# A fused mLSTM, token mixer and gated MLP on one core: the first two transfers are issued by ScalarE instead of SP

## The chip, the cores and the metric

The kernel runs on one core of one Trainium2 chip. The metric is the device time of one execution in microseconds (us). A core has TensorE (PE, whose weight loads are listed apart as PEld), VectorE (DVE), ScalarE (ACT), GpSimd (POOL) and SyncE (SP). Each has a queue of its own and works through it in order. Transfers between HBM and the core's memory (DMA) are issued by an instruction on an engine's queue and then run by themselves; whoever needs the data waits for a semaphore.

## The reference

Three stages on 2 sequences of 768 tokens, cut to what matters:

```python
# 1. mLSTM, 8 heads of 40: a recurrence with gates, in float32
for t in range(S):
    m_new = np.maximum(f_gate[:, :, t] + m, i_gate[:, :, t])
    f_stab, i_stab = np.exp(f_gate[:, :, t] + m - m_new), np.exp(i_gate[:, :, t] - m_new)
    m = m_new
    C = f_stab[..., None, None] * C + i_stab[..., None, None] * np.einsum('bhd,bhe->bhde', vt, kt)
    n = f_stab[..., None] * n + i_stab[..., None] * kt
    y[:, :, t] = sigmoid(o_gate[:, :, t]) * np.einsum('bhde,bhe->bhd', C, qt) / np.maximum(abs(n . qt), 1)
# 2. mixer: over tokens, then over channels
u  = x + (np.maximum(x.T @ w_tok1, 0) @ w_tok2).T
x2 = u + np.maximum(u @ w_ch1, 0) @ w_ch2
# 3. gated MLP: h = gelu(x2 @ w_in); u, v = halves of h; v normalized, mixed over tokens by w_sg
out = x2 + (u * (w_sg @ v_n + b_sg)) @ w_out
```

The mixer's weights come as float64 words and are made float32 on the chip.

## The kernel before, in words

The recurrence is done in chunks of 128 tokens, 6 for each of the 2 sequences, 12 in all (n = 0 to 11). First the gates of all chunks are worked out once (function gates): a scan on DVE over the f gates (L578), small transposes and matmuls on PE, and factors that are spread over heads (LR at L595 and L596, MR at L611). A chunk then has three parts. p1 makes the decay matrix E of 128 x 1024 in two halves: a matmul (L700), exp on ACT (L701), a mask on POOL (L702). p2 multiplies keys and queries on PE (L712) and the product with E on DVE (L713). p3 updates the carried state (L738, L743, L747, L751, L755), scales the queries with a row that is read back from DRAM (qs = wb x qk, L735; for chunk 1 from PE, L728) and makes the chunk's output (L761, L763, L764 to L768) in nat. The first token-mixing matmul of a chunk (L804) follows. After six chunks of a sequence come the second one (L836 to L838), transposes (L817, L820), and from about 95 us on the channel mixing and the gated MLP, long runs of matmuls.

Transfers: gates_in (gin: gates and small masks) and con (identity and masks) come first, both from one DRAM tensor (L544, L545). Each chunk loads qk in three pieces (L690 twice, L692) and kvo (L682), into three sets of buffers (qk, kvo: NSET = 3). Parts of the qk buffers that the transfers don't write are set to zero once at the start (L561 on DVE for the first set and on POOL for the others, L562 on POOL). wq goes out to DRAM once for each sequence (L650) and comes back in three pieces a chunk (wb, L733). Weights are loaded and converted in to_f32: the transfer (L499), ACT takes the absolute value (L503), DVE does four steps (L504 to L510), then ACT and POOL or DVE split it (L518, L519). rw__133 and rw__135 hold the first token weights, rw__136 and rw__138 the second.

The order on each queue isn't that of the code. Every operation is first recorded in a plan with an estimated cost; the planner simulates the engines from these estimates with several settings, takes the best of the orders that it finds, and issues that. A transfer is given an issue cost on its engine and a place in one common DMA queue; at most eight transfers are in flight, since each takes one of eight lanes (DMAHW0 to DMAHW7) and waits until the transfer eight before it has landed. Element-wise work marked flex may go to DVE or to POOL. Where the simulated PE would stand idle before it first uses a certain bank, the planner puts fillers there (matmuls on a constant, L576).

Of the kernel before, what the change touches and what calls it, by code (L numbers as in the profile page):

```python
# [424 lines left out]
def tile_mlstm_mixer_gmlp(  # L425
# [21 lines left out]
    pe, act, dve, pool, sp = (Engine(plan, e) for e in ("PE", "ACT", "DVE", "POOL", "SP"))  # L447
# [8 lines left out]
    def sb(name, col, n, dt=F32):  # L456

        t = nc.alloc_sbuf_tensor_at(name, [128, n], dt, offset=origin + 4 * col).ap()
        plan.base[t.tensor.name] = col
        return t  # L460
# [5 lines left out]
    con = sb("con", CON, 268)  # L466
# [74 lines left out]


    gates_in = r_gate.take("gin", 293)
    sp.dma_start(out=gates_in, in_=gates_d[:, 0:293])  # L544
    sp.dma_start(out=con, in_=gates_d[:, 293:561])  # L545
    fg, ig = gates_in[:, 0:128], gates_in[:, 128:256]
    ind12, neg, cap = gates_in[:, 256:268], gates_in[:, 268:269], gates_in[:, 269:270]
    ind6, hm = gates_in[:, 270:276], [gates_in[:, 276 + 8 * b:284 + 8 * b] for b in range(B)]
# [645 lines left out]
```

## Time and profile before

| | us |
|---|---|
| runs | 358.65, 359.51, 362.36 |
| median | 359.51 |
| profiled execution | 358.93 |
| its span, first to last instruction | 357.2 |
| PE busy | 350.1 (98%) |
| weight loads (PEld) busy | 337.8 (95%) |
| DVE, ACT, POOL busy | 258.0, 164.3, 96.2 |

The profiled execution is longer than its span by 1.7 us, which lie before the first and behind the last instruction. Busy times of one engine can include pipelining: a PE that is shown busy isn't at its peak. SPq, POOLq and so on stand for an engine's own queue, where transfers are issued and semaphores awaited. A buffer's number is left out of its name, so that wb stands for either of two buffers and ps for every bank of PSUM.

### The profile page before, as it was taken

The numbers are of one execution on the slowest core, as the hardware profiler recorded it, in microseconds if no ns is written. First come the engines' busy times: TensorE is split into PE (matmuls) and PEld (weight loads), VectorE is DVE, ScalarE is ACT, GpSimd is POOL, SyncE is SP. The second block draws the span as 40 slices with busy tenths as digits, with TensorE's granted clock in tenths as the row PEclk, the third lists the DMA queues.
The fourth block names the chain that finished last, engine by engine and source line by source line (L and its number), as shares of the span: only waits on it lengthen the run. The fifth ranks groups of instructions, "written<-read, shape, count | busy, mean of one in ns | idle before, by whom it ended". The sixth has DMA issues, their size and how long they took to land.

```text
span 357.2 us, 5949 instructions
## 1 busy us (share of the span) xinstructions
PE 350.1 (98%) x2238; PEld 337.8 (95%) x2238; DVE 258.0 (72%) x505; ACT 164.3 (46%) x367; POOL 96.2 (27%) x109
## 2 busy tenths in 40 slices
PE   8999999999999999999999999999999999999996
PEld 7889989989999999999999999999999999999995
DVE  5898789998896448981863468788799887455463
ACT  5677537864644235431442348545544544222230
POOL 4345337344223001110010005864231534000100
PEclk9999999999999999999999999999999999999999
DMA  5968777967900002001650000000000010010101
GB/s 155 322 199 305 229 230 263 306 235 237 333 4 0 2 9 111 0 3 44 242 171 0 2 1 2 0 0 2 1 2 0 0 57 0 2 56 1 57 0 55
DMA packets 12698, 32.47 MB, mean 91 GB/s; under 512 B 1766, under 2 KB 5694, under 8 KB 12670
## 3 DMA queue, kind: packets, MB, share of 16 engines
q1 hardware_dynamic: 12670, 32.10, 27.4%
q8 instruction: 17, 0.28, 0.3%
q14 instruction: 11, 0.09, 0.1%
HBM read 30.08 MB, written 2.02 MB: 90 GB/s over the span
## 4 chain that ended last, share of the span: by engine, by line
PE 81%; DMA 11%; DVE 3%; SPq 2%; issue 1%; POOL 1%; ACT 0%; DVEq 0%; POOLq 0%
PE ps L873 6%; PE ps L871 6%; PE ps L872 6%; PE ps L858 5%; PE ps L857 5%; PE ps L856 5%; PE ps L1028 5%; PE ps L1027 5%; PE ps L1026 5%; DMA qk<-in_qk_dram 4%; DMA rw__135<-in_tok_dram 4%; PE ps L763 2%; PE ps L861 2%; PE ps L860 2%; DMA rw__138<-in_tok_dram 2%; PE ps L1044 2%
## 5 line engine op out<-in xcount | busy, mean ns | idle before, releaser
L807 ACT ACTIVATE a<-ps 128x384 fp32r<-128x384 f32 x48 | 23.5, 491 | 53.6 <-PE ps L861 53.1
L808 DVE SCALAR_TENSOR_TENSOR a<-ps,a 128x384 fp32r<-128x384 f32 x48 | 26.6, 555 | 26.2 <-ACT a L807 25.7
L1028 PE MATMUL ps<-wsg,v 128*128 128x384 f32 x96 | 32.3, 336 | 0.0
L1026 PE MATMUL ps<-wsg,v 128*128 128x384 f32 x96 | 32.3, 336 | 0.0
L1027 PE MATMUL ps<-wsg,v 128*128 128x384 f32 x96 | 32.2, 336 | 0.0
L811 DVE TENSOR_TENSOR nat<-ps,nat 128x320 f32<-128x320 f32 x48 | 22.3, 489 | 13.8 <-PE ps L873 8.6
L712 PEld LDWEIGHTS ps<-qk 120*128 120x128 f32 (+1 forms) x192 | 24.9, 191 | 2.0 <-DVE nat L768 0.8
L712 PE MATMUL ps<-qk 120*128 120x128 f32 (+1 forms) x192 | 26.2, 275 | 0.5 <-DMA qk<-in_qk_dram 0.5
L1032 ACT CAST gs<-g 128x384 fp32r<-128x384 f32 x16 | 8.2, 512 | 37.2 <-DVE g L1031 37.2
L763 PE MATMUL ps<-kvo,E 128*128 128x41 f32 x192 | 23.2, 279 | 0.0
L702 POOL TENSOR_SCALAR_AFFINE_SELECT E<-E 128x512 f32<-128x512 f32 x24 | 17.9, 755 | 19.2 <-ACT E L701 18.1
L763 PEld LDWEIGHTS ps<-kvo,E 128*128 128x128 f32 x192 | 22.7, 192 | 0.0
L973 ACT ACTIVATE sq<-ps 128x384 f32<-128x384 f32 (+1 forms) x28 | 15.0, 535 | 14.5 <-PE ps L991 9.9
L974 DVE SCALAR_TENSOR_TENSOR sq<-sq,ps 128x384 f32<-128x384 f32 (+1 forms) x28 | 16.9, 608 | 6.5 <-ACT sq L973 6.0
L1030 DVE SCALAR_TENSOR_TENSOR g<-ps,gln,bsg 128x384 f32<-128x384 f32 x16 | 9.9, 617 | 15.5 <-PE ps L1028 15.5
L975 ACT ACTIVATE sq<-sq 128x384 f32<-128x384 f32 (+1 forms) x28 | 15.7, 568 | 9.8 <-DVE sq L974 9.5
L1028 PEld LDWEIGHTS ps<-wsg,v 128*128 128x128 f32 x96 | 18.0, 188 | 0.2 <-POOL v L1001 0.2
L1026 PEld LDWEIGHTS ps<-wsg,v 128*128 128x128 f32 x96 | 18.0, 188 | 0.0
L1027 PEld LDWEIGHTS ps<-wsg,v 128*128 128x128 f32 x96 | 18.0, 188 | 0.0
L824 DVE TENSOR_TENSOR uT<-ps,uT 128x384 fp32r<-128x384 f32 x24 | 13.3, 552 | 6.2 <-ACT uT L823 6.0
L701 ACT ACTIVATE E<-ps 128x512 f32<-128x512 f32 x24 | 14.2, 593 | 7.4 <-PE ps L700 6.2
L713 DVE TENSOR_TENSOR E<-ps,E 128x512 f32<-128x512 f32 x24 | 16.2, 683 | 2.0 <-PE ps L712 1.4
(351 smaller groups left out, 1118.4 us busy)
## 6 DMA issues: line engine op xcount, KB each, us to landing
kvo<-in_kvo_dram SPq DMA_DIRECT2D x12, 504.0 KB
qk<-in_qk_dram SPq DMA_DIRECT2D x36, 120.0 KB
rwin<-in_win_dram SPq DMA_DIRECT2D x5, 512.0 KB
rwsg<-in_wsg_dram SPq DMA_DIRECT2D x6, 384.0 KB
out_dram<-nat SPq DMA_DIRECT2D x12, 160.0 KB
rwo<-in_wout_dram SPq DMA_DIRECT2D x4, 320.0 KB
wb<-wq SPq DMA_DIRECT2D x18, 60.0 KB
rw__133<-in_tok_dram SPq DMA_DIRECT2D x1, 768.0 KB
```

What stands on the lines that cost most here:

```text
L702: pool.affine_select(out=E[:, hf], in_=E[:, hf], pattern=[[0, 4], [1, 128]], compare_op=ALU.is_ge, fill=0.0, base=0, channel_multiplier=-1)
L712: mm(p[:, j, :], kt[jj][0:r, g, :], qt[0:r, g, :], start=True, stop=True)
L763: mm(psO[:, h, :], E[:, h // 4, h % 4, :], v1[:, h, :], start=(c == 0 and h == 0), stop=(h == H - 1))
L807: act.activation(out=hi, in_=p, func=AF.Relu)
L808: dve.scalar_tensor_tensor(out=lo, in0=p, scalar=0.0, in1=asf(hi), op0=ALU.max, op1=ALU.subtract)
L811: dve.tensor_tensor(out=nat[:, b, s], in0=p, in1=nat[:, b, s], op=ALU.add)
L871: mm(acc, a[:, 0, js], w[:, 0, :], start=(m == 0), stop=False)
L872: mm(acc, a[:, 0, js], w[:, 1, :], start=False, stop=False)
L873: mm(acc, a[:, 1, js], w[:, 0, :], start=False, stop=(m == 5))
L1026: mm(p, v[:, 0, ds_], wsg[s][:, 0, ts], start=(s == 0), stop=False)
L1027: mm(p, v[:, 0, ds_], wsg[s][:, 1, ts], start=False, stop=False)
L1028: mm(p, v[:, 1, ds_], wsg[s][:, 0, ts], start=False, stop=(s == NC - 1))
```

## The change

Two lines name another engine for the issue.

```diff
     gates_in = r_gate.take("gin", 293)
-    sp.dma_start(out=gates_in, in_=gates_d[:, 0:293])
-    sp.dma_start(out=con, in_=gates_d[:, 293:561])
+    act.dma_start(out=gates_in, in_=gates_d[:, 0:293])
+    act.dma_start(out=con, in_=gates_d[:, 293:561])
```

Since the planner's simulation starts from other queues, it settles on another order for every engine. Three places show it.

**The start.** ACT's queue from its first instruction on, as a difference (+ is new):

```order
 L1189 UNCONDITIONAL_BRANCH
+L544 DMA gin<-in_gates_dram 128x293
+L545 DMA con<-in_gates_dram 128x268
 L581 ACT_TABLE_LOAD
 L581 ACTIVATE gt<-gt 128x128
```

The two transfers now stand ahead of the table load. SP's queue starts with the qk pieces of chunk 0 (L690 twice, L692), which stood third to fifth before, and its following issues keep their order up to the second piece of the fifth qk load. DVE's queue at the same place:

```order
 L1189 UNCONDITIONAL_BRANCH
-L561 MEMSET qk 120x384
 L575 MEMSET gt 128x128
 L626 MEMSET gt 1x1
+L561 MEMSET qk 120x384
 L578 SCALAR_TENSOR_TENSOR gt<-gt,gin 128x128
```

The zeroing of the first qk buffer, for which the first qk transfer waits, has moved behind the two memsets of the gates.

**The first chunk.** DVE's queue at the end of the gates' work, as a difference; L596 writes LR for the later chunks, L713 makes E of chunk 0, L611 spreads the factors for the chunks after it:

```order
 L652 TENSOR_SCALAR gt<-gin,gt 128x12
-L596 SCALAR_TENSOR_TENSOR LR<-LR,gin,ps 128x512
-L713 TENSOR_TENSOR E<-ps,E 128x512 x2
 L606 TENSOR_SCALAR gt<-gt 64x128
 L607 SCALAR_TENSOR_TENSOR gt<-gt 64x128
 L611 TENSOR_TENSOR MR<-gt,gin 128x512 x2
+L596 SCALAR_TENSOR_TENSOR LR<-LR,gin,ps 128x512
+L713 TENSOR_TENSOR E<-ps,E 128x512 x2
 L647 TENSOR_TENSOR wq<-gt,wq 64x128
```

L606, L607 and two L611 now come before L713. PE's queue over the same stretch, before:

```order
L655 MATMUL ps<-gt,selr 120x12 x3
L712 MATMUL ps<-qk 128x128 x10
L743 MATMUL ps<-wv,kvo 120x3x41 x2
L700 MATMUL ps<-MR,LR 128x512
L743 MATMUL ps<-wv,kvo 120x2x41
L763 MATMUL ps<-kvo,E 128x41 x4
```

and now:

```order
L655 MATMUL ps<-gt,selr 120x12 x3
L712 MATMUL ps<-qk 128x128 x4
L700 MATMUL ps<-MR,LR 128x512
L712 MATMUL ps<-qk 128x128 x2
L576 MATMUL ps<-gt 128x128 x3
L743 MATMUL ps<-wv,kvo 120x3x41
L700 MATMUL ps<-MR,LR 128x512
L743 MATMUL ps<-wv,kvo 120x3x41
L712 MATMUL ps<-qk 128x128 x4
```

The L712 work of chunks 0 and 1 is split, the first matmul for E (L700) comes earlier, and three fillers (L576) stand ahead of L743. Over the whole queue there are 10 fillers before and 17 now: one more at the start, these three, and three more ahead of the first L761.

**Weights and qs, some 25 to 50 us in.** SP's queue from rw__136 on, before:

```order
L499 DMA rw__136<-in_tok_dram 128x1536
L499 DMA rw__138<-in_tok_dram 128x1536
L650 DMA wq_87<-gt 8x6x128
L690 DMA qk<-in_qk_dram 40x768 x2
L692 DMA qk<-in_qk_dram 40x2x384
L733 DMA wb<-wq_86 40x256
L733 DMA wb<-wq_86 40x384 x2
L690 DMA qk<-in_qk_dram 40x768 x2
L692 DMA qk<-in_qk_dram 40x2x384
L682 DMA kvo<-in_kvo_dram 128x1008
```

and now, some ten rows behind rw__136:

```order
L682 DMA kvo<-in_kvo_dram 128x1008
L733 DMA wb<-wq_86 40x256
L733 DMA wb<-wq_86 40x384 x2
L690 DMA qk<-in_qk_dram 40x768 x2
L692 DMA qk<-in_qk_dram 40x2x384
L682 DMA kvo<-in_kvo_dram 128x1008
L499 DMA rw__138<-in_tok_dram 128x1536
L650 DMA wq_87<-gt 8x6x128
L690 DMA qk<-in_qk_dram 40x768 x2
L692 DMA qk<-in_qk_dram 40x2x384
L682 DMA kvo<-in_kvo_dram 128x1008
```

rw__138 and the second wq have moved back, behind three more qk loads, two kvo loads and six wb loads. POOL's queue over the same chunks, before:

```order
L755 TENSOR_TENSOR nb<-cd,ct 120x328
L702 AFFINE_SELECT E<-E 128x512 x2
L768 TENSOR_TENSOR nat<-tn,dn 128x320
L702 AFFINE_SELECT E<-E 128x512 x4
L738 TENSOR_TENSOR wv<-kvo,wT 128x328
L702 AFFINE_SELECT E<-E 128x512 x2
L735 TENSOR_TENSOR qs<-wb,qk 120x384
L702 AFFINE_SELECT E<-E 128x512 x2
```

and now:

```order
L755 TENSOR_TENSOR nb<-cd,ct 120x328
L702 AFFINE_SELECT E<-E 128x512 x2
L738 TENSOR_TENSOR wv<-kvo,wT 128x328
L735 TENSOR_TENSOR qs<-wb,qk 120x384
L702 AFFINE_SELECT E<-E 128x512 x3
L735 TENSOR_TENSOR qs<-wb,qk 120x384
L702 AFFINE_SELECT E<-E 128x512
L735 TENSOR_TENSOR qs<-wb,qk 120x384
L702 AFFINE_SELECT E<-E 128x512 x4
L735 TENSOR_TENSOR qs<-wb,qk 120x384
```

Of the nine qs operations (L735) eight were on DVE and one on POOL; now three are on DVE and six on POOL, between the masks L702. ACT's L503 on rw__138 stood behind the 12th L701 and the third L764, and now stands behind the 14th and the fifth.

## Rows read from the trace of the kernel before

**Rows 1.** the page, part 4: shares of the chain that ended last

```profile
PE 81%; DMA 11%; DVE 3%; SPq 2%; issue 1%; POOL 1%; ACT 0%; DVEq 0%; POOLq 0%
```

**Rows 2.** busy us by stretch: PE PEld DVE ACT POOL; clock, DMA share, GB/s

```profile
10.00:100.00 90.00, 88.01 (x660) 81.36 (x658) 80.58 (x155) 56.16 (x146) 36.44 (x41) 1.00 0.79 261
100.00:350.00 250.00, 250.00 (x1511) 244.96 (x1510) 170.20 (x327) 102.02 (x209) 54.92 (x56) 1.00 0.08 27
```

**Rows 3.** all that PE waited for: us in total, times, longest; six rows

```profile
PE ps L576 <- DVE gt L626: 1.5, 1, 1.5
PE ps L700 <- ACT E L701: 0.9, 3, 0.4
PE ps L712 <- DMA qk<-in_qk_dram: 0.5, 1, 0.5
...
PE ps L743 <- POOL wv L738: 0.2, 1, 0.2
```

**Rows 4.** groups of 0 to 100 us; then the chain, start us, us, what

```profile
L712 PEld LDWEIGHTS ps<-qk 120*128 120x128 f32 x144 | 20.4, 191 | 2.0 <-DVE nat L768 0.8
...
79.28 1.15 PE ps L804 x4
```

**Rows 5.** timeline, first 4 us: start, us, engine, line, operation [idle before]

```profile
0.78 1.28 ACT L581 ACT_TABLE_LOAD   x1 [0.78 <-PEq L1178]
...
0.79 0.38 SPq L544 DMA_DIRECT2D gin<-in_gates_dram  x1
0.94 0.38 DVE L561 MEMSET qk<- 120x384 f32 x1 [0.94 <-PEq L1178]
1.22 0.41 SPq L545 DMA_DIRECT2D con<-in_gates_dram  x1
1.29 0.17 DVE L575 MEMSET gt<- 128x128 f32 x1
...
1.68 0.74 SPq L690 DMA_DIRECT2D qk<-in_qk_dram  x2
2.08 0.31 ACT L581 ACTIVATE gt<-gt 128x128 f32<-128x128 f32 x1
...
2.46 0.94 SPq L692 DMA_DIRECT2D qk<-in_qk_dram  x1
...
3.14 0.42 DVE L578 TENSOR_TENSOR_SCAN gt<-gt,gin 128x128 f32<-128x128 f32 x1 [1.68 <-DMA gin<-in_gates_dram]
...
3.48 0.49 ACT L642 CAST selr<-con 128x360 fp32r<-128x360 f32 x1 [1.09 <-DMA con<-in_gates_dram]
```

**Rows 6.** timeline around chunk 0 on DVE and PE

```profile
11.94 0.69 DVE L713 TENSOR_TENSOR E<-ps,E 128x512 f32<-128x512 f32 x1 [0.42 <-PE ps L712]
...
13.11 1.80 DVE L611 TENSOR_TENSOR MR<-gt,gin 128x512 fp32r<-128x512 f32 x2
...
15.21 1.02 PE L763 MATMUL ps<-kvo,E 128*128 128x41 f32 x8
```

**Rows 7.** SP's queue: waits; then the chain between 4 and 45 us

```profile
SPq L690 <- DMA rw__138<-in_tok_dram: 2.6, 1, 2.6
...
27.53 7.53 DMA rw__138<-in_tok_dram
```

**Rows 8.** timeline of SP and of ACT around L503 on rw__138

```profile
38.46 0.36 SPq L682 DMA_DIRECT2D kvo<-in_kvo_dram  x1
...
43.70 0.18 ACT L764 ACTIVATE dn<-ps 128x8 f32<-128x8 f32 x1 [1.29 <-PE ps L763]
...
45.96 0.58 ACT L701 ACTIVATE E<-ps 128x512 f32<-128x512 f32 x1
```

**Rows 9.** tile wb: ns min/median/max, first, last start; who waited

```profile
L735 DVE TENSOR_TENSOR qs<-wb,qk x8: 551/558/980, 28.4 to 78.2; 120x384 f32<-120x384 f32 x8
...
L735 POOL TENSOR_TENSOR qs<-wb,qk x1: 1011/1011/1011, 51.8 to 51.8; 120x384 f32<-120x384 f32 x1
...
  DVE qs L735: 1.3, 2
```

## The prediction

> **What bounds the kernel now.** I read the chain of waits [rows 1], busy time by stretch [rows 2], all that PE waited for [rows 3], and then the timeline at the places that the change touches [rows 5 to 8]. 81% of the chain that ended last is PE. Behind 100 us PE is busy in 250.00 of 250.00 us and its weight loads in 244.96 [rows 2]: nothing that happens at the start can shorten that part, only begin it earlier or later. The granted clock is 1.00 in both stretches, so no term below is a clock term. The question is when PE gets through the first 100 us.
>
> How much could be won there? The named waits of PE are six and add up to 3.6 us, from 1.5 down to 0.2 [rows 3]; the 1.5 us stand before anything can run. That leaves 2.1 us.
>
> The Trainium skill ("Perfetto Trace Analysis", section "Identifying the Most-Contended Engine") warns against this reading: pipelined matmuls make TensorE's busy share a bad measure, and that of weight loads is to be used. The trace shows the difference: between 10 and 100 us PE has 88.01 of 90 us, the loads 81.36 [rows 2], so by that rule 8.6 us are open and not 2.1.
>
> From rows alone: 90 − 81.36 = 8.6 us without a load are no stall where a matmul takes longer than the next load. A load takes 0.191 us, an L804 matmul on the chain 1.15/4 = 0.29 [rows 4]; 48 of them hide 48 × 0.10 = 4.8 us. 3.8 us are left, the L700 matmuls still in it. So a reordering of the first 100 us gains 2.1 to 3.8 us at the very most: 1%, and only if every stall goes.
>
> **The change part by part.** The sum is made on the profiled execution: 358.93 us, 357.2 of span and 1.7 around it. The median of the three runs is 359.51, 0.6 higher.
>
> *SP loses two issues.* gin and con took 0.38 and 0.41 us there, and the first qk issue started at 1.68 [rows 5]; without them SP could start at 0.79. But that qk issue also waits for the DVE memset of its tile (L561), and the planner has moved this memset behind two others. From DVE's first start at 0.94, L575 (0.17), the one-element L626 and L561 (0.38) end near 1.55. SP starts some 0.1 us earlier, not 0.9, and its next 20 issues keep the old order; kvo of chunk 0 still waits for gin. Gain 0 to 0.1 us. That the change does not do what it says is thus part of my forecast.
>
> *ACT gets two issues ahead of its table load.* At SP's prices they end at 0.79 + 0.38 + 0.05 + 0.41 = 1.63, the load (1.28) at 2.91, the first ACTIVATE (0.31) at 3.22. L642, next on ACT, started at 3.48, when con had landed [rows 5]: 0.26 us to spare. gin is issued at the old time, so the DVE scan that waits for it stays at 3.14. Were an issue on ACT as dear as the dearest of these rows, 0.94, gin would leave 0.56 us later and con 1.09, and L642 with it. An issue that cost nothing would bring gin 0.4 us earlier. I take SP's figures, since they are for the same two transfers.
>
> What would a late gate chain cost? E of chunk 0 was ready at 11.94 + 0.69 = 12.63, and PE used it at 15.21 [rows 6], behind the work on kvo. The plan now puts L606, L607 (half a microsecond together by the gap of 12.63 to 13.11) and two L611 (1.80) ahead of both halves of E: 2.3 us, so E is ready near 14.9 and 0.3 us of cover are left. A chain late by 1.1 us costs 0.8; on time it costs nothing. Behind this cover every further microsecond counts in full.
>
> *A second DMA queue.* All issues before came from SP, so no trace shows ACT's queue. con may now share the DMA engines with qk. It landed 3.48 − 1.63 = 1.85 us after its issue; shared with one other transfer that could double, at the worst 1.85 us late, 1.5 us behind the cover. At the best it saves nothing, since it was first in line before. I take 0: qk is issued when con is already under way.
>
> The Trainium skill ("DMA: Bandwidth & Descriptors", section "Issuing engines are not separate DMA queues") says that transfers issued from any engine run on the same 16 DMA engines, and that several issuers save only sequencer time. By it the gain is at the most the 0.84 us of SP's issuing; no run here shows it yet.
>
> *The planner's new order.* This is the larger part: every engine is rearranged up to 100 us.
>
> First, seven more fillers (L576) stand in PE's queue, six of them among the work of chunks 0 to 2. Each makes two records; at one load each (0.191 [rows 4]) that is 6 × 2 × 0.191 = 2.3 us if none lies in a gap, and nothing if all do. The first three stand right in front of L743, which waited for wv before. I take +0.2.
>
> Second, rw__138 leaves SP seventeen issues behind rw__136 and not right behind it. Before, a qk issue waited 2.6 us for the lane that it held, and 7.53 us of the chain are its transfer [rows 7]. That wait goes. Late next is PE's own loop: there PE waited for E alone, 0.9 us in three times [rows 3]. So 0 to −0.9; I take −0.3. In exchange ACT's L503 on rw__138 now stands behind the fourteenth E and the fifth L764, which ran at 43.70 [rows 8]. The transfer is issued right behind kvo of chunk 6, at 38.46 before; with its 7.53 us it lands near 46. ACT would stand 2 us there, with two E's queued behind it, but the next E started only at 45.96 anyway. With L503's 0.9 us that E comes 1 us late: 0 to +1.0, and I take +0.2.
>
> Third, qs = wb × qk (L735): eight of nine were on DVE at 0.56 us, one on POOL at 1.01 [rows 9]; now three are on DVE and six on POOL. Five move: 5 × 0.45 = 2.3 us if each is on the path. Against that POOL has 53.6 of 90 us idle [rows 2] and DVE is relieved by 2.8 us. I take +0.3.
>
> The sum: 358.9 + 0 + 0.2 − 0.3 + 0.2 + 0.3 = 359.3. On the median's scale it is 359.9; I say **359.4 us**, a change too small to see.
>
> **The rivals.** *Faster, 356.8 us:* SP's queue is the limit of the first 50 us, and without the wait on rw__138 all named waits of PE behind the start vanish: 358.9 − 2.1. For it: the new order drops a link of 7.53 us from the chain. Against: PE waited for a transfer just once, 0.5 us [rows 3].
>
> *Slower, 365.1 us:* POOL's queue blocks. Each L735 waits for its wb transfers, and now the masks (L702) of later chunks' E stand behind it; where wb lands after ACT has finished that E, POOL stands, E is late, and PE with it. The price is the 2.3 us above and the wait that DVE had for wb, 1.3 us in two cases [rows 9], 0.65 each, six times: 3.9. Together 358.9 + 6.2. For it: POOL works in order, and five of the six stand directly ahead of an L702. Against: with rw__138 out of the way wb lands earlier, and E is made several chunks ahead.
>
> *ACT late, 360.2 us:* issues on ACT cost 0.94 each, the gate chain is 1.1 us late, and the forecast's 359.4 grows by 0.8. For it nothing in the rows but that no issue on ACT was ever seen; against it that SP's issues of the same shape took 0.4.
>
> The Trainium skill ("ScalarE: Activation LUTs", section "What ACT_TABLE_LOAD costs") counts a drain of about 1.38 us to each load; by it L642 would come some 1.1 us late, the same 360.2. The trace speaks against it: the load began at 0.78, took 1.28, and the ACTIVATE began at 2.08 [rows 5].
>
> **How the numbers follow.** The three runs spread over 3.7 us, so about 1% is what a measurement of this kernel tells from no change. The forecast, within 1.5 us of 359.4, gets 0.70, the faster rival 0.10, the blocked POOL 0.13, ACT late 0.07. Faster by over 1%, under 355.9, needs every stall of the larger count to go: 0.05. Over 363.1 lies most of the POOL case, and a little of the fillers on top of another loss: 0.12. Within 1%: 0.83. The range goes from the faster rival, 356.8, to 363.2, where fillers and half of the POOL price would come together; the rest of the POOL case is left out.
>
> **What would show it.** Right: the first qk issue near 1.6, L642 near 3.5, PE's first L763 near 15.2, the qk issue near 33 without its wait, PE's named waits still some 2 us behind the start, and the same 245 us of loads in the last 250. Wrong: L642 after 4.3, so that ACT's issue is dear; L702 late behind an L735 that waits for wb, with PE's wait for E over 3 us in sum; ACT standing at L503 beyond 47. The forecast fails if PE reaches its first steady stretch, near 95 us, more than 3 us earlier or later than before.

## The result, and the profile after

The changed kernel takes 361.26 us (median of 20 runs, 358.53 to 368.2), the kernel before 358.01 beside it (20 runs). The ratio is 1.0071, 95% interval 1.0048 to 1.0093: slower, by 1.7 to 3.3 us. The forecast of 359.4 said no change; the median lies in its range, and 0.71% in its "within 1%", but it is a change that a measurement does tell from none. The median lies in the range by the range's width, which is luck, and not by the sum, which gave 0.4 us. The comparison leaves disturbed executions out, and the profiled one of the changed kernel (365.42 us, span 363.6) is one of these; it shows the loss larger than it is on average.

First the start, on the timeline of the changed kernel (start, us, engine, line, operation):

```profile
0.78 0.39 ACTq L544 DMA_DIRECT2D gin<-in_gates_dram  x1
...
1.20 0.45 ACTq L545 DMA_DIRECT2D con<-in_gates_dram  x1
1.52 0.75 SPq L690 DMA_DIRECT2D qk<-in_qk_dram  x2
1.68 1.28 ACT L581 ACT_TABLE_LOAD   x1 [1.68 <-PEq L1178]
...
2.97 0.31 ACT L581 ACTIVATE gt<-gt 128x128 f32<-128x128 f32 x1
...
3.18 0.42 DVE L578 TENSOR_TENSOR_SCAN gt<-gt,gin 128x128 f32<-128x128 f32 x1 [1.68 <-DMA gin<-in_gates_dram]
...
3.48 0.49 ACT L642 CAST selr<-con 128x360 fp32r<-128x360 f32 x1 [0.20 <-DMA con<-in_gates_dram]
```

Against [rows 5] this is as forecast: two issues at SP's price (0.39 and 0.45 us), SP's first qk 0.16 us earlier, the scan at the same time, L642 at 3.48 as before. The start isn't where time is lost. All that PE waited for, as [rows 3] has it for before:

```profile
PE ps L700 <- ACT E L701: 3.8, 1, 3.8
PE ps L576 <- DVE gt L575: 1.1, 1, 1.1
PE ps L761 <- DVE qs L728: 0.9, 1, 0.9
PE ps L817 <- DVE nat L811: 0.2, 1, 0.2
```

Three waits for E of 0.9 us together have become one of 3.8, and 0.9 for L728 is new. The timeline around the long one, SP's rows first:

```profile
38.86 0.41 SPq L682 DMA_DIRECT2D kvo<-in_kvo_dram  x1
39.32 0.42 SPq L499 DMA_DIRECT2D rw__138<-in_tok_dram  x1
39.78 0.68 SPq L650 DMA_DIRECT2D wq<-gt  x1
...
48.59 2.17 SPq L733 DMA_DIRECT2D wb<-wq  x6
...
43.61 0.18 ACT L764 ACTIVATE dn<-ps 128x8 f32<-128x8 f32 x1 [1.58 <-PE ps L763]
...
45.44 0.50 DVE L738 TENSOR_TENSOR wv<-kvo,wT 128x328 f32<-128x328 f32 x1 [3.30 <-PE ps L700]
48.42 0.90 ACT L503 ACTIVATE wt<-rw__138 128x768 f32<-128x768 f32 x1 [4.64 <-DMA rw__138<-in_tok_dram]
49.22 0.58 ACT L701 ACTIVATE E<-ps 128x512 f32<-128x512 f32 x1
49.85 0.79 PE L700 MATMUL ps<-MR,LR 128*128 128x512 f32 x1 [3.85 <-ACT E L701]
...
52.93 3.34 PE L763 MATMUL ps<-kvo,E 128*128 128x41 f32 x15
```

rw__138 is issued at 39.32 and lands at 48.42, after 9.1 us instead of 7.53 [rows 7]. ACT stands 4.64 us at L503, the E behind it comes at 49.22 (before: 45.96, [rows 8]), and PE stands. Two more engines stand in the same stretch: DVE at L738 until 45.44, and SP, whose six wb wait for wq until 48.59. (The releaser that the DVE row names had been done long before; in e0 and e2 below the same row names kvo.) Busy time by stretch, columns as in [rows 2]:

```profile
40.00:50.00 10.00, 6.15 (x49) 5.61 (x47) 6.59 (x14) 3.19 (x9) 2.15 (x4) 0.93 0.79 234
50.00:60.00 10.00, 10.00 (x45) 9.04 (x45) 5.49 (x10) 1.72 (x5) 2.35 (x4) 0.55 0.48 144
60.00:100.00 40.00, 39.69 (x305) 37.11 (x304) 36.17 (x70) 26.67 (x69) 17.51 (x17) 1.00 0.76 254
100.00:350.00 250.00, 250.00 (x1514) 244.93 (x1513) 175.57 (x337) 104.21 (x216) 49.40 (x53) 1.00 0.10 35
```

Behind the pause the granted clock is 0.55 for ten us, the lower of its two levels (1.2 of 2.4 GHz) for most of them, and 15 L763 take 3.34 us. The last stretch is as before: 244.93 us of loads, 244.96 in [rows 2].

Where PE is at the end of the recurrence tells how much is lost by then. Its last group of L804 but one, before (first row) and after (second):

```profile
93.85 0.70 PE L804 MATMUL ps<-nat,w__134 128*128 128x320 f32 x2
```

```profile
100.53 0.70 PE L804 MATMUL ps<-nat,w__134 128*128 128x320 f32 x2
```

From there to the end it is 357.2 − 93.85 = 263.35 us before and 363.6 − 100.53 = 263.07 after. So the whole loss is ahead of this mark, in every run below but e7. The mark is used for all of them.

### The profile page after: what moved, and what is told of

The parts are those of the page before. It is cut to its first block, busy times and chain, and to the rows that moved or that the text cites. A ratio compares the mean times of both kernels' runs of the same rounds, so it can differ in the third digit from the quotient of the medians.

```text
span 363.6 us, 5982 instructions
## 1 busy us (share of the span) xinstructions
PE 354.0 (97%) x2252; PEld 342.3 (94%) x2252; DVE 262.9 (72%) x507; ACT 163.3 (45%) x367; POOL 91.2 (25%) x107
## 4 chain that ended last, share of the span: by engine, by line
PE 87%; DMA 5%; DVE 4%; issue 1%; SPq 1%; ACT 1%; ACTq 0%; DVEq 0%
PE ps L873 6%; PE ps L871 6%; PE ps L872 6%; PE ps L858 5%; PE ps L857 5%; PE ps L856 5%; PE ps L1028 5%; PE ps L1027 5%; PE ps L1026 5%; PE ps L763 4%; PE ps L712 3%; PE ps L804 3%; PE ps L860 2%; PE ps L861 2%; DMA rc__147<-in_ch_dram 2%; PE ps L1044 2%
## 5 line engine op out<-in xcount | busy, mean ns | idle before, releaser
L811 DVE TENSOR_TENSOR nat<-ps,nat 128x320 f32<-128x320 f32 x48 | 22.3, 490 | 15.4 <-PE ps L873 8.5
L712 PEld LDWEIGHTS ps<-qk 120*128 120x128 f32 (+1 forms) x192 | 25.7, 196 | 1.5 <-issue 0.2
L712 PE MATMUL ps<-qk 120*128 120x128 f32 (+1 forms) x192 | 26.6, 280 | 0.0
L763 PE MATMUL ps<-kvo,E 128*128 128x41 f32 x192 | 24.8, 290 | 0.0
L763 PEld LDWEIGHTS ps<-kvo,E 128*128 128x128 f32 x192 | 24.3, 204 | 0.0
L702 POOL TENSOR_SCALAR_AFFINE_SELECT E<-E 128x512 f32<-128x512 f32 x24 | 16.7, 705 | 29.3 <-ACT E L701 29.2
L713 DVE TENSOR_TENSOR E<-ps,E 128x512 f32<-128x512 f32 x24 | 15.9, 681 | 4.9 <-PE ps L712 4.2
L701 ACT ACTIVATE E<-ps 128x512 f32<-128x512 f32 x24 | 14.2, 591 | 6.6 <-PE ps L700 5.8
```

Source lines behind the costliest of these rows:

```text
L712: mm(p[:, j, :], kt[jj][0:r, g, :], qt[0:r, g, :], start=True, stop=True)
L763: mm(psO[:, h, :], E[:, h // 4, h % 4, :], v1[:, h, :], start=(c == 0 and h == 0), stop=(h == H - 1))
L811: dve.tensor_tensor(out=nat[:, b, s], in0=p, in1=nat[:, b, s], op=ALU.add)
```

## The experiments

All edits act on the order that the planner returns, or on its settings. Where a kernel edits the order, `issue()` runs through `self.edited(self.best())` instead of `self.best()`, and the diff shows what `edited` does to the list `ops` (one list for all engines; each engine's row is its part of it). Ratios are to the kernel before, run beside them; the mark is the start of PE's last group of L804 but one in the profile (93.85 before). The diffs are shortened: words in place of code, and remarks behind #, are not in the kernels.

### The issuing engine, or the order

**e0**, the changed kernel again. 

> The changed kernel itself, once more, beside the next three. Both theories: 1.005 to 1.009 times the kernel before. Late-load theory (the loss is ACT standing at L503 for rw__138): PE's L700 near 50 us waits 3 to 4 us for an E of L701, and ACT stands 4 to 5 us at the L503 ahead of that E. If the granted clock falls below 1.00 only in the 20 us behind that pause and nowhere else, the clock is a consequence of it. Issuing theory (the loss is ACT's issues or the second queue): the pause is there in some executions and not in others, at the same total time.

Measured: 1.0080 (1.0046 to 1.0114). In its profile PE waits 2.8 us for E, ACT stands 3.57 us at L503, both a little under what was expected, and the clock is 0.51 from 50 to 60 us and 1.00 behind it.

**e1**, the order of before, the two issues on ACT:

```diff
+    for o in ops:
+        if o.line in (544, 545):
+            o.eng = "ACT"
```

> The order of the kernel before on every engine; only the issues of gin and con move from SP to ACT. Late-load theory: 0.997 to 1.002 times the kernel before, rw__138 landed by 36, no wait of PE over 1.5 us behind the start. Issuing theory: 1.005 to 1.009, as the whole change.

Measured: 0.9993 (0.9959 to 1.0027). The issuing engine and the second queue cost nothing that shows, by the interval at most 1 us.

**e2**, the changed kernel's order, the two issues on SP (base: the changed kernel):

```diff
+    for o in ops:
+        if o.line in (544, 545):
+            o.eng = "SP"
```

> The order of the changed kernel on every engine; gin and con are issued by SP again, ahead of its other transfers. Late-load theory: 1.005 to 1.010 times the kernel before, with PE's wait of 3 to 4 us near 50. Issuing theory: 0.997 to 1.002.

Measured: 1.0054 (1.0015 to 1.0093), as the late-load theory said, but with a wait for E of 1.8 us and not of 3 to 4. PE's waits and ACT's row in e2:

```profile
PE ps L817 <- DVE nat L811: 2.0, 2, 1.7
PE ps L700 <- ACT E L701: 1.8, 1, 1.8
...
46.08 0.90 ACT L503 ACTIVATE wt<-rw__138 128x768 f32<-128x768 f32 x1 [2.63 <-DMA rw__138<-in_tok_dram]
```

The order alone makes the loss. With a clock of 1.00 throughout, PE is at the mark at 95.69, 1.8 us late. Where it fell behind, before first and then e2:

```profile
63.12 1.32 PE L804 MATMUL ps<-nat,w__132 128*128 128x320 f32 x4
...
66.25 0.41 PE L817 MATMUL ps<-con,nat 128*128 128x128 f32 x2
```

```profile
63.08 1.32 PE L804 MATMUL ps<-nat,w__132 128*128 128x320 f32 x4
...
68.13 0.41 PE L817 MATMUL ps<-con,nat 128*128 128x128 f32 x2 [1.72 <-DVE nat L811]
```

At 63 us PE is level with before, so in this profile the wait for E is made up; the 1.8 us come behind it, when L817 waits for DVE's L811. L811 ran at 67.50, and at 65.62 before. Ahead of it on DVE, at 63.03, stands the L519 on the weights of rw__138, which ran on POOL before; no run moved it alone.

**Why the order is another.** The planner tries 24 settings in two rounds each and keeps the order with the lowest estimate of its own. These are its estimates (no times of the chip), as the code works them out for both kernels; the columns are the largest element-wise operation for POOL, margin, how many us ahead of its due time a transfer may go, round, estimate:

```
before:  999  0.0   32  second  357.21   taken
         999  0.15  20  first   358.50
after:   999  0.0   32  second  360.33
         999  0.15  20  first   358.46   taken
```

The order that it had taken is gone: under the same setting the plan now comes out 3.1 worse by its own count, and the runner-up, which had been there all along, is taken. Held to this setting, the planner of the kernel before writes the order of e2, row for row on every engine. So the new order isn't made by the two issues: the planner draws again, and takes one that it had before. The shorter reach, 20 us and not 32, isn't enough to make rw__138 and wq_87 late: with 20 us, margin 0.0 and the second round the planner of the kernel before leaves rw__138 right behind rw__136.

### Single steps of the new order

**e3**, rw__138 right behind rw__136 (base here and up to e11, but for e5: the changed kernel):

```diff
+    loads = [the transfers of rw__136 and rw__138]
+    ops.remove(loads[1])
+    ops.insert(ops.index(loads[0]) + 1, loads[1])
```

> The changed kernel with one issue moved: SP issues rw__138 right behind rw__136, eighteen places earlier; all else stays. Late-load theory: ACT no longer stands at the L503 on rw__138, PE's wait near 50 is under 1 us, the granted clock stays 1.00, and the time is 0.996 to 1.002 times the kernel before (2 to 4 us under the changed kernel). Rival (fillers, POOL's qs or the 0.9 us at L761 make the loss): 1.004 to 1.009, as before the edit.

Measured: 1.0133 (1.0080 to 1.0185). The theory of the late load, as it stood, falls. ACT's stand is gone, another has come. From e3's timeline and its list of PE's waits:

```profile
37.70 1.01 POOL L735 TENSOR_TENSOR qs<-wb,qk 120x384 f32<-120x384 f32 x1 [5.42 <-DMA qk<-in_qk_dram]
...
38.74 0.66 SPq L690 DMA_DIRECT2D qk<-in_qk_dram  x2
...
40.36 0.41 SPq L682 DMA_DIRECT2D kvo<-in_kvo_dram  x1
...
45.53 0.50 DVE L738 TENSOR_TENSOR wv<-kvo,wT 128x328 f32<-128x328 f32 x1 [5.37 <-DMA kvo<-in_kvo_dram]
...
PE ps L761 <- DVE nb L755: 1.3, 1, 1.3
...
50.00:60.00 10.00, 10.00 (x52) 8.66 (x52) 9.93 (x16) 4.57 (x12) 5.67 (x5) 0.72 0.46 141
```

SP's next qk issue waits 2.2 us for rw__138, POOL's qs is late by qk, SP's next qk by qs (it waits for the buffer), kvo behind it 1.5 us later than in the changed kernel; DVE stands 5.37 us at L738 with L755 behind it, and PE waits for that. The clock falls here too, to 0.72.

**e4**, ACT's L503 on rw__138 behind the next two L701 (and DVE's L504 on its result behind two L713):

```diff
+    ops.remove(first)                        # L503 on rw__138
+    ops.insert(ops.index(late) + 1, first)   # the second L701 behind it
+    ops.remove(b)                            # L504 on its result
+    ops.insert(ops.index(c), b)              # right ahead of its L505
```

> The changed kernel; rw__138 stays late in SP's queue, but ACT's L503 on it stands behind the next two L701 instead of ahead of them, and DVE's L504 on its result behind the two L713 that follow. Late-load theory as it stands after the early-load run: PE's wait for E near 46 to 50 falls under 1 us; what is late next there is DVE's L738, which waits for kvo with L755 behind it (44 to 46), so PE may still wait up to 1 us for nb at L761. Time 0.998 to 1.004 times the kernel before, 1.5 to 3 us under the changed kernel. Rival (kvo and DVE's row are as late as rw__138, so taking ACT's stand away only shows the other): PE waits 1.3 us or more for nb or wv, and the time stays at 1.005 to 1.009.

Measured: 1.0098 (1.0059 to 1.0137), so that the rival is the nearer, though PE waits 0.8 us for nb and not the 1.3 that it named. PE's waits in e4:

```profile
PE ps L817 <- DVE nat L811: 1.6, 2, 1.3
...
PE ps L700 <- ACT E L701: 1.1, 1, 1.1
PE ps L761 <- DVE nb L755: 0.8, 1, 0.8
```

**e5**, the kernel before with rw__138 and its L503, L504, L505 late:

```diff
+    ops.insert(ops.index(kvo) + 1, words)    # behind the seventh kvo
+    ops.insert(ops.index(fifth_L764) + 1, a) # its L503
+    ops[k + 1:k + 1] = [b, c]                # L504, L505 behind a later L738
```

> The kernel before with rw__138 alone moved as the change moves it: issued behind the seventh kvo, ACT's L503 on it between the fifth L764 and the E that follows, DVE's L504 and L505 on it later too. Late-load theory: ACT stands 2 to 4 us at that L503, PE waits 1 to 4 us for E near 46 to 50, and the time is 1.003 to 1.010 times the kernel before, with the granted clock under 1.00 behind the pause in some executions. Rival (the loss needs the rest of the new order): 0.997 to 1.002.

Measured: 1.0027 (0.9979 to 1.0076), which tells nothing apart. In its profile rw__138 was issued at 36.05 already, and ACT stood 0.18 us, not the 2 to 4 wanted, so the dose wasn't given.

**e6**, e3, and DVE's L738 behind the L755:

```diff
+    ops.remove(wv)
+    ops.insert(ops.index(nb) + 1, wv)
```

> The early load of e3 with one more step: DVE's L738, which waited 5.4 us for kvo there, stands behind the L755 on which PE's L761 waited. If both loads in front of an engine's queue are the loss (ACT's on rw__138, DVE's on kvo): PE's wait at L761 near 46 falls from 1.3 to under 0.5 us, the granted clock stays 1.00, and the time is 0.997 to 1.004 times the kernel before. Rival (SP is 1.5 us late with all that follows, whatever stands first on DVE): PE waits as long for wv or E instead, and the time stays above 1.008.

Measured: 1.0162 (1.0104 to 1.0221). As the rival said, PE goes through 46 without a wait, and waits 1.8 us for E at 60 instead.

**e9**, without the six fillers:

```diff
+    fill = [o for o in ops if o.line == 576][11:]
+    ops = [o for o in ops if o not in fill]
```

> The changed kernel without the six fillers of L576 among chunks 0 to 2 (they write nothing that is read). If the fillers cost what the prediction took as their upper end: 2.3 us less than the changed kernel, 0.999 to 1.003 times the kernel before. If they lie in PE's slack, as PE's pause near 46 to 50 says: 1.004 to 1.010, the same pause; a lower granted clock ahead of 40 would say that they hold the clock up.

Measured: 1.0079 (1.0045 to 1.0113), the 1.0080 of e0: no cost of the fillers shows. In its profile there is no pause at 46 (L817 waits 1.2 us at 73 instead), so the fixed place that the expectation named isn't one. The clock did fall ahead of 40, to 0.79 from 25 to 30 us, behind a wait of 0.8 us for L728; it did so too in e14, with the fillers in (0.68), so that this isn't put down to them.

**e10**, DVE's L738 on POOL, as in the kernel before; **e11**, this and e4:

```diff
+    wv.eng = "POOL"
```

> The changed kernel with one step of DVE, the L738 that stood 2.9 to 5.4 us for the seventh kvo near 41 to 45 in its profiles, on POOL, as in the kernel before; all other rows stay. In-line theory (both ACT at L503 and DVE at L738 stand in line for a late transfer, and taking one away leaves the other): DVE's idle time between 40 and 50 falls by 2 us or more, PE's wait for E near 46 to 50 stays, and the time is 1.003 to 1.008 times the kernel before. Rival (DVE's stand alone is what is paid back behind 50): 0.998 to 1.002. Rival (any hand edit of this order only moves the wait): 1.006 or more, with a new wait of PE elsewhere.

> The step of e10 and that of e4 together: L738 of the seventh kvo on POOL, ACT's L503 on rw__138 behind the next two L701, DVE's L504 on it behind the two L713. In-line theory: no wait of PE over 0.8 us between 40 and 55, granted clock 1.00, and 0.998 to 1.003 times the kernel before. Rival (SP's row is late as a whole; wq_87 behind rw__138 holds the next six wb): 1.005 or more, with SP's L733 waiting 2 us or more for wq_87 and PE's waits between 55 and 70 instead.

Measured: 1.0068 (1.0038 to 1.0098) and 1.0101 (1.0053 to 1.0148). In e10 PE waits 1.0 us for E and 2.2 us at a new place, L817, which the in-line theory and the second rival both allow. PE's waits in e10:

```profile
PE ps L817 <- DVE nat L811: 2.4, 2, 2.2
...
PE ps L700 <- ACT E L701: 1.0, 1, 1.0
```

In e11 PE is busy in 15.00 of 15.00 us from 40 to 55, and then, from its timeline:

```profile
49.68 2.23 SPq L733 DMA_DIRECT2D wb<-wq  x6
...
52.50 0.50 DVE L738 TENSOR_TENSOR wv<-kvo,wT 128x328 f32<-128x328 f32 x1 [4.27 <-DMA kvo<-in_kvo_dram]
...
57.91 1.34 PE L804 MATMUL ps<-nat,w__134 128*128 128x320 f32 x4 [2.34 <-DVE nat L768]
...
62.59 0.50 PE L700 MATMUL ps<-MR,LR 128*128 128x512 f32 x1 [1.76 <-ACT E L701]
```

With both taken out of line the stand moves to the next kvo and to the wb behind wq, as the rival said, and PE pays 4.1 us at 58 and 62. No step tried is the cause by itself.

### Rows and settings

**e7**, the compute engines' rows of the changed kernel, SP's row of the kernel before, joined engine by engine; **e16**, the same rows, joined so that the list keeps the changed kernel's order wherever it can:

```diff
+    seq["SP"] = [SP's operations in the order of the kernel before]
...
+        o = min((o for o in head if all(q in put for q in o.pre + o.hold)), key=at.get)
+        ops.append(o)
```

> The changed kernel's order on PE, DVE, ACT and POOL, and on SP the order of the kernel before (gin and con still from ACT): rw__138 and wq_87 leave right behind rw__136, and the seventh kvo leaves ahead of the qk that stood before it. SP theory (the loss sits in SP's row as a whole: rw__138, wq_87 and kvo late, and moving rw__138 alone only makes the others later): no wait of PE over 1 us between 40 and 70, granted clock 1.00, 0.997 to 1.003 times the kernel before. Rival (the rows of the compute engines make it: L735 on POOL holds a buffer of qk, L738 on DVE stands ahead of L755): PE still waits 1.5 us or more in sum between 40 and 70, and the time is 1.004 to 1.016.

> The question of e7 once more, with the two orders joined so that no wait comes in that neither kernel has: PE, DVE, ACT and POOL as in the changed kernel, row by row, SP as in the kernel before. If SP's row makes the loss of the stretch from 25 to 60: 0.997 to 1.003 times the kernel before. If the compute rows of the stretch make it: 1.004 to 1.010. If rows only fit together (the compute rows were laid out for transfers in the new order): above 1.010.

Measured: e7 1.0451 (1.0392 to 1.0510), e16 1.0100 (1.0052 to 1.0148). e7 says nothing of SP: PE waited six times, 3.3 us, for ACT at L743, a wait that other kernels have for 0.4 us at most, and 4.9 us for rwin. In e16 PE waits 1.8 us for E at 60. SP's row of before doesn't help the other rows of the changed kernel.

**e8**, the change, the planner held to the setting that it took before:

```diff
-    rounds=2, windows=(16.0, 20.0, 25.0, 32.0), margins=(0.0, 0.15, 0.3), bigs=(400, 999)
+    rounds=2, windows=(32.0,), margins=(0.0,), bigs=(999,)
```

> The change, with the planner held to the setting that it had picked for the kernel before (transfers up to 32 us ahead of their due time, no margin, second round) in place of the one that it picks now (20 us, margin 0.15, first round). gin and con from ACT; the order is new again on all engines, but rw__138 and wq_87 leave early. If the setting is what makes the loss: 0.996 to 1.003 times the kernel before, PE's named waits behind the start 2 us or less. Rival (the old order was the lucky one of many, and any other loses): 1.004 to 1.012, with PE's waits at other places.

Measured: 1.0137 (1.0105 to 1.0169). rw__138 leaves at 18.64 here and PE waits for L811 and E all the same (1.9 and 1.4 us). The setting isn't the cause. Of the three orders, the planner's estimates of 357.21, 358.46 and 360.33 stand in the order of the times, 1, 1.0071 and 1.0137.

### In which stretch

**e12 to e15 and e17**: the two orders cut at a time of the planner's clock and joined crosswise:

```diff
+    head = [(o, e) for o, e, s in mine if s < 25.0]
...
+    rest = [the operations of the other plan that are not in head]
+    ops = head + rest     # each with its engine in that plan
```

e12 is new to 25 us, then old; e13 old to 25, then new; e14 and e15 the same at 60; e17 is new, with 25 to 60 old.

> Grafted orders, cut at 25 us of the planner's own clock: what the changed kernel's plan starts before 25, as it stands there (gin and con from ACT, the new start, the fillers), then all the rest in the order of the kernel before. If the loss lies behind 25 (rw__138, wq_87, kvo and the rows around them): 0.997 to 1.003 times the kernel before. If it lies in the first 25 us and only shows later: 1.004 to 1.010. If any new order loses: 1.004 or more, in e13 as well.

> The opposite graft: the kernel before up to 25, then the order of the changed kernel. If the loss lies behind 25: 1.004 to 1.010. If it lies in the first 25 us: 0.997 to 1.003.

> The changed kernel's order up to 60 us, then that of the kernel before. If the loss lies between 25 and 60, where PE first fell behind in the profiles: 1.004 to 1.010. If it is made or paid behind 60: 0.997 to 1.003.

> The kernel before up to 60 us, then the order of the changed kernel. If the loss lies between 25 and 60: 0.997 to 1.003. If it is made behind 60 (DVE's row near 65 to 73, where PE waited for L811 in four profiles): 1.004 to 1.010.

> The changed kernel with only the stretch of 25 to 60 us, on all engines, in the order of the kernel before; gin and con from ACT, the new start and the new end stay. If the loss lies in that stretch: 0.997 to 1.004 times the kernel before, no wait of PE over 1.5 us between 40 and 75, executions with a granted clock under 0.995 as rare as in the kernel before. If the first 25 us make it: 1.004 to 1.010.

| | to 25 us | 25 to 60 | behind 60 | ratio | interval | mark in the profile |
|---|---|---|---|---|---|---|
| e0 | new | new | new | 1.0080 | 1.0046 to 1.0114 | 100.45 |
| e12 | new | old | old | 1.0036 | 1.0004 to 1.0068 | 94.46 |
| e17 | new | old | new | 1.0039 | 1.0009 to 1.0069 | 95.09 |
| e13 | old | new | new | 1.0035 | 0.9989 to 1.0081 | 95.25 |
| e14 | new | new | old | 1.0180 | 1.0105 to 1.0254 | 97.03 |
| e15 | old | old | new | 0.9979 | 0.9950 to 1.0008 | 94.24 |

With the old rows ahead of 60 the new ones behind it cost nothing (e15), so the loss needs the new rows ahead of 60, though part of it can be paid behind (e2, at 68). How it divides between the first 25 us and 25 to 60 isn't settled. By the middle values each has half: 0.0036 to 0.0039, some 1.3 us, for the first 25 us (e12, e17), and 0.0041 (e0 against e17) or 0.0035 (e13) for the rest. But the intervals overlap; e12 and e13 lie between what was named for either case, and e17 lies within what was named for a loss in 25 to 60 alone. A seam can cost by itself, too: e14 is worse than the whole. And the profiles of the whole new order show no loss near 43 us, where PE starts a group of L804 at 43.34 (after), 43.20 (e0) and 43.01 (e2), and at 43.43 before. PE's waits in e12:

```profile
PE ps L700 <- ACT E L701: 1.2, 1, 1.2
...
PE ps L761 <- DVE qs L728: 0.8, 1, 0.8
```

The wait for L728 near 20 us stands in six of the fourteen profiles with the new start (after, e9, e11, e12, e14 and, at 0.3, e17) and in none with the old. It is a candidate for the first half, no more: e0 and e2 lose without it, and no run took it away alone. e12 and e15 also pause for E, 1.2 us at 53.67 and 1.4 at 46.67, where before did for 0.4 at most. In e15 all rows up to there are those of the kernel before, and PE came to them 1 us earlier: a wait of this size in one profile need not be a loss.

## Why the prediction was wrong

**The engine and the start: right.** ACT's issues cost what SP's did (0.39 and 0.45 us), L642 stayed at 3.48, and the second queue cost nothing that shows: e1, 0.9993. "ACT late" and "SP's queue is the limit" are out. PE's first L763 came at 14.17 and not near 15.2; kvo's first reader, ACT's L720, ran at 11.05 and not at 12.91. The lead was spent again by 21 us (L728, below).

**The fillers:** taken at +0.2 of 0 to 2.3; e9 shows no cost, and its interval leaves no room for 2.3.

**rw__138's wait gone, −0.3:** the wait went, the gain didn't show. At the last group of L804 ahead of the pause PE was at 43.34 after and 43.43 before.

**In exchange, ACT's L503 on rw__138, +0.2 of 0 to +1.0: the step that failed.** The place was right, the size wrong: PE waited 3.8, 2.8 and 1.8 us there (after, e0, e2). "It lands near 46" took the 7.53 us of [rows 7] for a property of the transfer; it took 6.3 us in e2, 8.7 in e0 and 9.1 in after. And "the next E started only at 45.96 anyway" had no slack behind it: that E was what PE waited for. What the term left out is more: in the same ten us SP stood for wq and DVE for kvo, so that with L503 out of the way PE waits elsewhere (e4, e11). The sum priced one stand with all other rows on time. Nor is this wait the whole: in e2 PE had made it up by 63 us, and was late by L817's wait of 1.7 us for L811, for which the sum had no term. In place of the sum's 0.4 us for the new order the runs show 1.7 to 3.3 for it as a whole; how they divide among its rows stays open.

**qs on POOL, +0.3:** no wait of PE names it. It is a link in e3's chain (38.74 behind 37.70 on POOL), and by itself it wasn't tried. The rival "POOL's queue blocks" named PE's wait for E over 3 us as its sign; the sign came, but the row at 48.42 puts it on L503, not on a mask behind L735.

**A term that wasn't there:** the wait of up to 0.9 us for L728, which makes chunk 1's qs. On DVE's timeline of the changed kernel, and PE's row behind it:

```profile
18.24 1.08 DVE L504 TENSOR_SCALAR wt<-wt 128x768 f32<-128x768 f32 x1
19.35 0.56 DVE L505 TENSOR_SCALAR wt<-wt 128x768 int32<-128x768 int32 x1
19.95 0.96 DVE L507 SCALAR_TENSOR_TENSOR wt<-rw__133,wt 128x768 int32<-128x768 int32 x1
20.82 0.55 DVE L728 TENSOR_TENSOR qs<-ps,qk 120x384 f32<-120x384 f32 x1
...
21.43 0.79 PE L761 MATMUL ps<-nb,qs 120*128 120x123 f32 x5 [0.88 <-DVE qs L728]
```

Three weight steps, 2.6 us, stand ahead of L728 here; before they stood behind it (L728 at 19.17, L504 at 21.55). The prediction looked at E of chunk 0 at this place, said 14.9, and there was no loss (its last L713 ended at 13.23, before at 12.63).

**"No term below is a clock term"** was read from a trace without a long pause. In the profile of after the clock adds some 3 us to what the pause costs: PE went from 43.34 to 56.27 between two groups of L804, 12.93 us, and from 43.43 to 49.75 before, 6.32: 6.6 us more, of which 3.85 are the pause. But the clock isn't needed for the loss: the 8 of 12 executions of e0 with a mean clock of 0.998 or more have a median of 360.42, the 24 of 29 of the kernel before beside them 357.49.

**What stays open:** which rows of the new order make the loss, whether the first 25 us have a part in it, and whether any order close to the new one would be free of it. Shown is that the order alone makes it, that it needs the new rows ahead of 60 us, and that no step tried on its own takes it away.

## What to carry to other kernels

Where a planner searches for an order, a small edit isn't small: it draws a new order, and the old one was the best of many draws. Both new draws here (after, e8) were slower, though the edit by itself cost nothing that shows. So compare what the planner says of its own new choice with what it said of the old one, and test the edit with the order held. A stand on an in-order queue is priced with the transfers that are late beside it, not one at a time, and a transfer's time from issue to landing isn't fixed (6.3 to 9.1 us for rw__138). Follow PE beyond a wait before calling the wait the loss: in e2 it was made up. A pause can be followed by a lower clock (0.55 for ten us in after).

## What the runs showed of the hardware that was not expected

**The clock.** By stretches of five us, the granted clock fell behind the start in eleven of the twenty profiles, each time where PE had paused: to 0.50 at the 3.85 us of after, the 2.8 of e0, the 1.8 of e6 and e16 and the 1.3 of e3, to 0.65 at the 4.9 of e7, to 0.80 and 0.82 at the 2.3 of e11 and the 2.2 of e10, to 0.72 at 0.8 in e4, and to 0.68 and 0.79 at 0.7 and 0.8 near 22 us in e14 and e9. The reverse doesn't hold: 1.8 and 1.7 us in e2, 1.9 in e8, 1.5 in e13 and 1.4 in e15 and e17 were followed by 1.00. Over all executions the mean clock was under 0.995 in 7 of 20 of the changed kernel, 4 of 12 of e0 and 5 of 12 of e2, in 20 of the 122 of the kernel before beside e0 to e17, and in none of 36 of e12, e15 and e17.

**A small transfer behind a large one.** wq, 24 KB, was issued 0.46 us behind rw__138's 768 KB in the changed kernel, and SP could go on with wb only 8.8 us later (39.78 to 48.59), at the time when rw__138 landed (48.42). In e0 and e2 it was the same: rw__138 landed at 47.21 and 46.08, and SP went on at 47.25 and 46.32. In the list of SP's waits of the changed kernel:

```profile
SPq L733 <- DMA wq<-gt: 4.4, 1, 4.4
```

**Issues ahead of the table load.** ACT issued two transfers before its first ACT_TABLE_LOAD, and the ACTIVATE still began right behind the load (1.68 + 1.28 = 2.96; 2.97).
